# RWKV-6 attention followed by a leaky-ReLU MLP: a written-out order of all steps in place of a list scheduler

## The chip, the cores and the metric

The kernel runs on one core of a Trainium2 chip. The metric is device time in microseconds (us) from one launch to its end; lower is better. Three runs of the kernel before took 179.11, 179.33 and 179.73 us.

## What is computed

The input is a linear attention with a decaying state (4 batches, 8 heads, 768 positions, 48 channels per head), and its output, seen as 3072 tokens of 384 channels, goes through a two-layer MLP with a leaky ReLU between:

```python
for t in range(S):
    cur = np.einsum('bhd,bhe->bhde', u[None] * kt, vt)
    y[:, :, t] = np.einsum('bhd,bhde->bhe', rt, state + cur)
    state = wt[:, :, :, None] * state + np.einsum('bhd,bhe->bhde', kt, vt)
...
h = x @ w_in                      # (3072, 384) @ (384, 2048)
g = np.maximum(0.01 * h, h)
return (g @ w_out).astype(np.float32)   # (3072, 2048) @ (2048, 384)
```

## The kernel before, in words

**Tiling.** The positions are cut into chunks of 128 (24 in all, 6 for each batch). The first two chunks of batches 0 and 1 are done as two "pairs" (`pair`, chunks 0 and 1, then 2 and 3): a pair loads w, k, r and v of 256 positions with one DMA each (384 KB). All later chunks are "singles" (`single`), with four loads of 192 KB. A chunk takes the logarithm of its decays (ACT), sums them along the positions with a triangular matmul (PE), takes exponentials (ACT), scales r and k (DVE), transposes them, either on PE with a copy back or by a DMA transpose (`RK_DMA`), multiplies them (the "scores"), masks the scores (DVE, `m`), and multiplies them with v (PE, "intra"). v is cast on POOL (`vb`); POOL also makes the bonus term of u (`ru`, then `vs`). For a pair the bonus is added on PE (L808, `add_vs`). The result `y` is transposed into `xT`, the MLP's input.

**The MLP.** Chunks are joined in blocks (`blocks`, of one or two chunks). A block has "up" steps (L1157, `up`: six matmuls of 256 columns or twelve of 128, into one PSUM bank, then the leaky ReLU into `g` on ACT, L1183) and "down" steps (L1196, four matmuls of 384 columns each, four steps a chunk). The last three blocks use a seven-product scheme for their down part (`seven`, L1098). The weights arrive as float32 and are cast to bf16 by POOL, ACT or DVE (L478): `w_in` as parts in0 to in3 (384 KB each), in4 and in6 (768 KB each, two casts each), `w_out` as out0, out2, out4 and out6 (768 KB each, two casts each).

**The order of the work.** Every piece above is a "step": a closure with the engines it may run on and their planned durations, the steps it depends on, and the buffers it takes and reads. There are 1092 of them, numbered as they are made. `Plan.order` is a list scheduler: it walks through planned time, and whenever an engine is free it gives it the ready step of the lowest rank whose buffers can be had. The ranks are a base value plus an entry of `RANK`, a table of 1090 numbers; `FORCE` fixes the engine of some steps. A step's planned end is prolonged by `SLACK` (0.2 us) for most steps of the attention. The steps are then issued in the order of the plan; on the chip, each engine works through its own steps strictly in that order and waits for the others by semaphores. SyncE (SP) issues all large DMAs, in its own order too. In the first 24 us of planned time, gaps of PE are filled with matmuls on a tile of zeros (L1240).

**Buffers.** One buffer `xT` holds the transposed activations of all 24 chunks. Loads and weights go through ten `in` buffers, `g` has three, and the transposed r and k of a pair (`rkT2`) have two of their own. PSUM has eight banks (`ps`).

```python
xT = pool.tile([128, KT, NCH * L], BF16, name="xT")
make("in", 10, [128, 1536], F32)
make("rkT2", 2, [128, 2 * NP, 256], BF16)
make("g", 3, [128, NJ, max(blocks) * L], BF16)
```

Of the kernel before, what the change touches and what calls it, by code (L numbers as in the profile page):

```python
# [23 lines left out]
class Plan:  # L24


    ENGINES = ("PE", "DVE", "ACT", "POOL", "SP")
# [4 lines left out]
    def __init__(self, limits, slack_from, slack, late):  # L32
        self.steps, self.limits, self.late = [], limits, late
        self.slack_from, self.slack = slack_from, slack
# [8 lines left out]
    def order(self, pools):  # L43
        n = len(self.steps)
        users = [[] for _ in range(n)]
        left = [len(s[3]) for s in self.steps]
        for i, s in enumerate(self.steps):
            for j in s[3]:
                users[j].append(i)
        bufs = {}  # L50
        for i, s in enumerate(self.steps):
            for b in (*s[4], *s[5]):
                bufs[id(b)] = b
        remain = {k: len(b.users) for k, b in bufs.items()}
        free_tiles = {p: [(0.0, k) for k in range(len(t))] for p, t in pools.items()}
        in_use = {}
        ready_at = [0.0] * n
        self.start, self.done, self.eng = [None] * n, [0.0] * n, [None] * n
        free = dict(self.BEGIN)
        ready = {e: [] for e in self.ENGINES}  # L60
        events = []
        dma_free, flying = 0.0, []

        def offer(i, t):
            for e in self.steps[i][0]:
                heapq.heappush(events, (t, 0, e, i))

        for i in range(n):
            if not left[i]:
                offer(i, 0.0)  # L70
        for e in self.ENGINES:
            heapq.heappush(events, (free[e], 1, e, -1))
        count, out = 0, []
        while events:
            now, kind, e, i = heapq.heappop(events)
            same = {e}
            if kind == 0 and self.start[i] is None:
                heapq.heappush(ready[e], (self.steps[i][2], i))
            elif kind == 2:
                in_use[i] -= 1  # L80
            while events and events[0][0] <= now + 1e-9:
                _, kind, e, i = heapq.heappop(events)
                same.add(e)
                if kind == 0 and self.start[i] is None:
                    heapq.heappush(ready[e], (self.steps[i][2], i))
                elif kind == 2:
                    in_use[i] -= 1
            for e in self.ENGINES:
                if (e not in same and "*" not in same) or free[e] > now + 1e-9:
                    continue  # L90
                held, chosen = [], None
                while ready[e]:
                    pri, i = heapq.heappop(ready[e])
                    if self.start[i] is not None:
                        continue
                    want, ok = {}, True
                    for b in self.steps[i][5]:
                        if b.t is None:
                            want[b.pool] = want.get(b.pool, 0) + 1
                            if in_use.get(b.kind, 0) >= self.limits.get(b.kind, 99):  # L100
                                ok = False
                    for p, k in want.items():
                        if sum(f <= now + 1e-9 for f, _ in free_tiles[p]) < k:
                            ok = False
                    if ok:
                        chosen = i
                        break
                    held.append((pri, i))
                for h in held:
                    heapq.heappush(ready[e], h)  # L110
                if chosen is None:
                    continue
                i = chosen
                engs, fn, pri, deps, reads, takes, wire = self.steps[i]
                for b in takes:
                    if b.t is None:
                        slots = free_tiles[b.pool]
                        s = min(slots)
                        slots.remove(s)
                        b.slot = s[1]  # L120
                        b.t = pools[b.pool][s[1]]
                        in_use[b.kind] = in_use.get(b.kind, 0) + 1
                d = engs[e]
                self.start[i], self.eng[i] = now, e
                out.append(i)
                count += 1
                free[e] = now + d - (self.OVER[e] if d > 0.3 else 0.0)
                if wire is None:
                    self.done[i] = now + d + self.SEEN[e]
                    if self.slack_from <= pri < 1000:  # L130
                        self.done[i] += self.slack
                else:
                    wire, size, lat, lead = wire
                    while flying and sum(x for _, x in flying) + size > 150:
                        free[e] = max(free[e], flying.pop(0)[0])
                    dma_free = max(dma_free, free[e] + lead) + wire
                    flying.append((dma_free, size))
                    self.done[i] = dma_free + lat + (self.late if now > 20 else 0.0)
                heapq.heappush(events, (free[e], 1, e, -1))
                for j in users[i]:  # L140
                    left[j] -= 1
                    ready_at[j] = max(ready_at[j], self.done[i])
                    if not left[j]:
                        offer(j, ready_at[j])
                for b in {id(b): b for b in (*reads, *takes)}.values():
                    b.free_at = max(b.free_at, self.done[i])
                    remain[id(b)] -= sum(u == i for u in b.users)
                    if remain[id(b)] == 0:
                        free_tiles[b.pool].append((b.free_at, b.slot))
                        heapq.heappush(events, (b.free_at, 2, "*", b.kind))  # L150
        if count != n:
            raise RuntimeError(("stuck", count, n, [(self.steps[i][0], self.steps[i][2]) for i in range(n) if self.start[i] is None][:20]))
        return out
# [9 lines left out]
RANK = {0: -309.63, 1: -310.62, 2: -303.35, 3: -175.12, 4: -176.12, 5: -3.85, 6: -313.07, 7: -303.34, 8:  # L163
# [148 lines left out]
def kernel(  # L312
# [27 lines left out]
    MERGED = {6, 10, 12, 14, 16, 18, 20}  # L340
    LEAD = 4
    AHEAD = 4
    SLACK_FROM = 50
    SLACK = 0.2
    LATE = 0.0
    WARM_UNTIL = 24.0
# [61 lines left out]
    with tc.manual_schedule():  # L408
# [817 lines left out]
        for i, e in FORCE.items():  # L1226
            plan.steps[i][0] = {e: plan.steps[i][0][e]}
# [47 lines left out]
```

## Time and profile before

| | |
|---|---|
| three runs | 179.11, 179.33, 179.73 us (median 179.33) |
| profiled execution, first to last instruction (span) | 177.7 us; the median run is 1.6 us above it |
| busy share of the span | PE 96%, PE weight loads 75%, DVE 75%, ACT 65%, POOL 59% |
| chain that ended last | PE 74%, DMA 8%, SP's queue 5%, ACT 4%, DVE 3% |
| read from HBM, written to it | 25.17 MB, 4.72 MB |

PE is TensorE, ACT ScalarE, DVE VectorE, POOL GpSimd. PE's weight loads overlap its matmuls. A matmul's record is longer than the time until the next one starts, since matmuls are pipelined, so a busy share near 100% says that PE was never empty, not that it could do no more; the pace is read from the chain, where each piece ends with the start of the next.

### The profile page before, as it was taken

To read this page: it belongs to the slowest core of one execution; us is meant where nothing else is said; L and a number is where in the kernel's file an instruction comes from. 1 tells how busy PE (TensorE), PEld (TensorE's weight loads), DVE (VectorE), ACT (ScalarE), POOL (GpSimd) and SP (SyncE) were. 2 spreads that over 40 slices of the span, in tenths; PEclk is the share of its full clock that TensorE was granted. 3 is DMA by queue.
4 is the path that set the end of the run, shared out by engine and by line. 5 is a ranking of instruction groups with operands and counts; after the bars stand their busy time and mean duration, and the time that the engine had idled before them with its cause. 6 is when DMAs were issued, how large, how long until landed. Compare 5 with 4: busy or idle time off the path is not lost.

```text
span 177.7 us, 5379 instructions
## 1 busy us (share of the span) xinstructions
PE 170.7 (96%) x2106; PEld 133.9 (75%) x2110; DVE 133.9 (75%) x268; ACT 115.6 (65%) x258; POOL 105.3 (59%) x139
## 2 busy tenths in 40 slices
PE   7899899999999999999999999999999999999993
PEld 2456678766879767797788776788777798899992
DVE  7599744568987949979968888699779688776463
ACT  5679877764856687487497891288873677662820
POOL 5998554255897749993905994659884099100000
PEclk9999999999999999999999999999999999999999
DMA  5999999999999999997999999997999996613004
GB/s 142 262 283 341 338 377 325 234 197 168 193 146 210 171 189 191 194 227 171 221 185 209 197 147 222 205 177 155 191 208 148 241 207 160 159 24 111 4 22 157
DMA packets 115884, 34.24 MB, mean 193 GB/s; under 512 B 108305, under 2 KB 115090, under 8 KB 115858
## 3 DMA queue, kind: packets, MB, share of 16 engines
q1 hardware_dynamic: 115856, 33.89, 94.3%
q8 instruction: 16, 0.26, 0.7%
q14 instruction: 10, 0.08, 0.2%
q10 hardware_dynamic: 2, 0.00, 0.0%
HBM read 25.17 MB, written 4.72 MB: 168 GB/s over the span
## 4 chain that ended last, share of the span: by engine, by line
PE 74%; DMA 8%; SPq 5%; ACT 4%; DVE 3%; issue 3%; POOL 1%; DVEq 0%; ACTq 0%; POOLq 0%
PE ps L1168 29%; PE ps L1198 23%; PE ps L1098 8%; DMA in<-in_moe_w_in_dram 5%; SPq L630 4%; DMA in<-in_w_dram 3%; PE ps L1002 3%; PE ps L973 2%; ACT g L1183 2%; PE ps L861 2%; PE ps L556 2%; PE ps L968 2%; PE ps L942 1%; PE ps L604 1%; DVE in L1048 1%
## 5 line engine op out<-in xcount | busy, mean ns | idle before, releaser
L1168 PE MATMUL ps<-xT,w_in_b 128*128 128x256 bf16 (+1 forms) x720 | 73.3, 251 | 0.1
L1183 ACT ACTIVATE g<-ps 128x512 bf16<-128x512 f32 x96 | 55.9, 594 | 22.4 <-PE ps L1168 19.5
L1168 PEld LDWEIGHTS <-w_in_b 128*128 128x128 bf16 x720 | 57.6, 98 | 8.4 <-issue 0.3
L1198 PE MATMUL ps<-w_out_b,g 128*128 128x384 bf16 x288 | 56.5, 326 | 0.0
L1198 PEld LDWEIGHTS <-g 128*128 128x128 bf16 x288 | 25.1, 97 | 12.0
L545 DVE TENSOR_TENSOR rk<-in,ps 128x384 bf16<-128x384 f32 x48 | 25.3, 550 | 8.0 <-ACT ps L887 3.0
L575 POOL TENSOR_TENSOR ru<-in,ub 128x384 f32<-128x384 f32 x24 | 25.4, 1061 | 6.2 <-DMA in<-in_k_dram 6.1
L932 DVE TENSOR_TENSOR m<-ps,maskb 128x512 bf16<-128x512 f32 x40 | 25.3, 682 | 4.2 <-PE ps L1002 3.3
L595 POOL CAST vb<-in 128x384 bf16<-128x384 f32 x24 | 13.2, 553 | 22.3 <-DMA in<-in_v_dram 19.1
L579 POOL TENSOR_TENSOR ru<-ru,in 128x384 f32<-128x384 f32 x24 | 24.4, 1028 | 2.9 <-DMA in<-in_r_dram 2.4
L587 POOL TENSOR_TENSOR vs<-in,dg 128x384 f32<-128x384 f32 x20 | 17.0, 852 | 3.5 <-DVE dg L583 2.9
L919 POOL TENSOR_TENSOR sb<-s,a 128x384 bf16<-128x384 f32 x18 | 14.9, 830 | 3.3 <-ACT a L882 3.3
L873 DVE TENSOR_TENSOR ci<-ps,lw 128x384 f32<-128x384 f32 x20 | 11.1, 553 | 4.5 <-PE ps L861 1.8
L618 DVE TENSOR_TENSOR y<-ps,vs 128x384 bf16<-128x384 f32 x20 | 10.9, 553 | 4.5 <-PE ps L973 4.5
L583 DVE TENSOR_REDUCE dg<-ru 128x8 f32<-128x384 f32 x24 | 13.1, 544 | 0.7 <-POOL ru L579 0.6
L882 ACT ACTIVATE a<-ps 64x4 f32<-64x4 f32 x36 | 6.1, 168 | 11.6 <-DVE ci L873 8.9
L855 ACT ACTIVATE lw<-in 128x384 bf16<-128x384 f32 x20 | 10.1, 520 | 3.8 <-DMA in<-in_w_dram 3.6
L891 ACT ACTIVATE ps<-ci 128x384 f32<-128x384 f32 x20 | 9.7, 485 | 1.8 <-DVE ci L873 1.8
L887 ACT ACTIVATE ps<-ps 128x384 f32<-128x384 f32 x20 | 9.3, 467 | 0.5 <-DVE ci L873 0.3
L1240 PE MATMUL ps<-zeros 128*128 128x128 bf16 (+1 forms) x31 | 7.6, 351 | 1.6 <-DVE zeros L409 1.3
L556 PE MATMUL ps<-ident,rk 128*128 128x128 bf16 x88 | 8.4, 220 | 0.5 <-DVE rk L545 0.4
L1098 PEld LDWEIGHTS <-g 128*128 128x128 bf16 x96 | 8.1, 98 | 0.2
(105 smaller groups left out, 222.5 us busy)
## 6 DMA issues: line engine op xcount, KB each, us to landing
out_dram<-o SPq DMA_DIRECT2D x23, 192.0 KB, 2.7
in<-in_w_dram SPq DMA_DIRECT2D x20, 192.0 KB, 4.6
in<-in_v_dram SPq DMA_DIRECT2D x20, 192.0 KB, 4.9
in<-in_r_dram SPq DMA_DIRECT2D x20, 192.0 KB, 4.4
in<-in_k_dram SPq DMA_DIRECT2D x20, 192.0 KB, 4.6
in<-in_moe_w_out_dram SPq DMA_DIRECT2D x4, 768.0 KB, 8.7
in<-in_moe_w_in_dram SPq DMA_DIRECT2D x4, 384.0 KB, 7.8
in<-in_moe_w_in_dram SPq DMA_DIRECT2D x2, 768.0 KB, 8.5
```

Source lines behind the costliest of these rows:

```text
L545: (nc.gpsimd if e == "POOL" else nc.vector).tensor_tensor(out=o, in0=x, in1=i, op=ALU.mult)
L575: lambda e: nc.gpsimd.tensor_tensor(out=ru.t[:], in0=kv(), in1=ubv, op=ALU.mult),
L579: lambda e: nc.gpsimd.tensor_tensor(out=ru.t[:], in0=ru.t[:], in1=rv(), op=ALU.mult),
L583: lambda e: nc.vector.tensor_reduce(out=dg.t[:], in_=ru.t[:], axis=AX.X, op=ALU.add),
L587: lambda e: nc.gpsimd.tensor_tensor(out=vs.t[:], in0=vv(), in1=dg.t[:].unsqueeze(2).to_broadcast([128, H, D]), op=ALU.mult),
L595: {"POOL": 0.56}, lambda e: nc.gpsimd.tensor_copy(out=vb.t[:], in_=vv()),
L919: lambda e: nc.gpsimd.tensor_tensor(out=sb.t[:].rearrange("p g a d -> p (g a) d"), in0=s_in.t[:].rearrange("p g a d -> p (g a) d"), in1=a_ ...
L932: lambda e, par=par: nc.vector.tensor_tensor(out=m.t[:, par, :, :], in0=sc[par].t[:].rearrange("p (g t) -> p g t", g=NP), in1=maskb[:].uns ...
L1098: nc.tensor.matmul(o(), lhsT=x()[:, i, :], rhs=y()[:, i, :], start=fresh, stop=(stop and i == ii[-1]), skip_group_check=True)
L1168: nc.tensor.matmul(hp.t[:, a * N : (a + 1) * N], lhsT=w_in_b[:, t, (j + a) * 128 : (j + a + 1) * 128], rhs=xT[:, t, c0 : c0 + N], start=(a ...
L1183: lambda e, hp=hp, g=g, j=j, J=J, N=N: nc.scalar.activation(out=g.t[:, j : j + J, 0:N], in_=hp.t[:, 0 : J * N].rearrange("p (a n) -> p a n ...
L1198: nc.tensor.matmul(op.t[:, 0:DM], lhsT=g.t[:, j, off : off + 128], rhs=w_out_b[:, j, :], start=(j == 0), stop=(j == NJ - 1))
```

## The change

The list scheduler goes. `RANK` and `SLACK` are removed; a list `ORDER` names all 1092 steps in the order in which they are issued, and `FORCE` (64 entries before, 93 after) their engines where there is a choice. `Plan.order` only walks through `ORDER`, keeps the planned times (which decide which of several free buffers a step gets, and how many matmuls on zeros fill PE's early gaps), and hands the list back. Some planned durations are altered, which alters nothing on the chip by itself.

`xT` becomes six buffers of one block each, taken by the step that writes a block's first chunk and free again after the block's last up step. `rkT2` has no buffers of its own and uses `g`'s, of which there are four. `in` has eleven buffers.

```diff
-    def __init__(self, limits, slack_from, slack, late):
+    def __init__(self, limits):
...
+        for i in ORDER:
+            engs, fn, deps, reads, takes, wire = self.steps[i][0], *self.steps[i][1:2], *self.steps[i][3:]
+            if left[i]:
+                raise RuntimeError(("before its inputs", i))
+            e = FORCE.get(i) or next(iter(engs))
+            now = max(at[e], ready[i])
+            for b in takes:
+                if b.t is None:
+                    slot = min(free[b.pool])
...
+                    now, b.slot, b.t = max(now, slot[0]), slot[1], pools[b.pool][slot[1]]
...
-RANK = {0: -309.63, 1: -310.62, 2: -303.35, 3: -175.12, 4: -176.12, 5: -3.85, 6: -313.07, 7: -303.34, 8:
...
+ORDER = [0, 1, 4, 2, 3, 1090, 5, 6, 7, 11, 14, 20, 12, 18, 19, 13, 21, 15, 16, 17, 8, 25, 22, 36, 40, 26, 27,
...
-    xT = pool.tile([128, KT, NCH * L], BF16, name="xT")
-    make("in", 10, [128, 1536], F32)
+    make("in", 11, [128, 1536], F32)
-    make("rkT2", 2, [128, 2 * NP, 256], BF16)
-    make("g", 3, [128, NJ, max(blocks) * L], BF16)
+    make("g", 4, [128, NJ, max(blocks) * L], BF16)
+    make("xT", 6, [128, KT, max(blocks) * L], BF16)
...
+        for nb, size in enumerate(blocks):
+            xb = Buf("xT")
+            for off in range(size):
+                place[len(place)] = (xb, off * L)
...
-            return step({"ACT": 0.48, "DVE": 0.36}, xcopy, P0 + 1, deps=[s_yt], reads=[yp])
+            return step({"ACT": 0.48, "DVE": 0.36}, xcopy, P0 + 1, deps=[s_yt], reads=[yp], takes=[place[n][0]])
...
-            rkT = Buf("rkT2")
+            rkT = Buf("g", "rkT2")
...
-                                rhs=xT[:, t, c0 : c0 + N], start=(a == 0 and t == 0),
+                                rhs=xb.t[:, t, 0:N], start=(a == 0 and t == 0),
```

What this makes of the first part of each engine's queue, in short names: w0 to v0 are the loads of the first pair, w2 to v2 those of the second, w4 and so on those of single chunks; in0 to out6 are loads of weights on SP and their casts elsewhere (in4b is the second cast of in4); "b1 j8" is the up step of block 1 that begins with the 128 columns numbered 8; "down q0" is the first quarter of a chunk's down part.

| queue | before | after |
|---|---|---|
| SP, from the start | w0 k0 r0 v0 w2 in0 k2 r2 in4 in2 v2 in1 in3 out0 in6 out2 w4 out4 out6 v4 r4 k4 w5 | w0 k0 r0 w2 v0 k2 r2 in0 in4 v2 in1 in2 in3 in6 out0 w4 out2 out4 out6 k4 r4 w5 k5 v4 |
| POOL, from `vs` of the first pair | vs vs, in0, ru ru ruk ruk of the second pair, in4, vb2 vb2 vs2 vs2, in3, out0, in6, out2, out4 | vs vs, ru ru ruk ruk, in0, vb2 vb2 vs2 vs2, in1, in2, in6, out0b, out2b, out4 |
| ACT, from the second pair's exponentials | copies and casts of rkT, y and xT; in4b, g, in2, g g, in1, g, y y, g g | y y, two rkT, xT xT, in4, in4b, g g g, state, y, in3, g, in6b, g g g, out0, ln of chunk 4 |
| DVE, from the second pair's masks | four masks, dg, sb, state, xT, out0b, in6b, out2b, ci4, out4b, out6b | four masks, sb, y, xT xT, ci4, out2, out4b, out6b |
| PE, from b0 j0 | j0, j10, j8, pp2, j4, intra2, add2, bonus2, inter2, j2, yT, j6, yT, b1 j8 ... | j0, j8, pp2, j10, intra2, add2, bonus2, inter2, j2, yT, j4, yT, b1 j8 ... |

The first 61 entries of PE's queue are the same steps in both, in another order; the 61st is the same step in both, the last quarter of chunk 1's down part. Across the whole kernel DVE gets nine steps fewer and ACT nine more; PE, POOL and SP keep the number of theirs.

More of the change, by code (lines that the diff above doesn't have):

```diff
@@ L43, in order @@
     def order(self, pools):
-        n = len(self.steps)
-        users = [[] for _ in range(n)]
         left = [len(s[3]) for s in self.steps]
+        users = [[] for _ in self.steps]
         for i, s in enumerate(self.steps):
@@ L49, in order @@
                 users[j].append(i)
-        bufs = {}
-        for i, s in enumerate(self.steps):
+        remain, free = {}, {p: [(0.0, k) for k in range(len(t))] for p, t in pools.items()}
+        for s in self.steps:
             for b in (*s[4], *s[5]):
[L53 to L150, printed above, removed]
@@ L151, in order @@
-        if count != n:
-            raise RuntimeError(("stuck", count, n, [(self.steps[i][0], self.steps[i][2]) for i in range(n) if self.start[i] is None][:20]))
-        return out
+                remain[id(b)] = len(b.users)
+        n = len(self.steps)
+        self.start, self.done, self.eng, ready = [None] * n, [0.0] * n, [None] * n, [0.0] * n
+        at, in_use, wire_free, flying = dict(self.BEGIN), {}, 0.0, []
+        for i in ORDER:
[7 more added lines that the diff above has]
+                    slot = min(free[b.pool])
+                    free[b.pool].remove(slot)
+                    in_use[b.kind] = in_use.get(b.kind, 0) + 1
+                    if in_use[b.kind] > self.limits.get(b.kind, 99):
+                        raise RuntimeError(("too many", b.kind, i))
+                    now, b.slot, b.t = max(now, slot[0]), slot[1], pools[b.pool][slot[1]]
+            self.start[i], self.eng[i] = now, e
+            at[e] = now + engs[e] - (self.OVER[e] if engs[e] > 0.3 else 0.0)
+            if wire is None:
+                self.done[i] = now + engs[e] + self.SEEN[e]
+            else:
+                time, size, lat, lead = wire
+                while flying and sum(x for _, x in flying) + size > 150:
+                    at[e] = max(at[e], flying.pop(0)[0])
+                wire_free = max(wire_free, at[e] + lead) + time
+                flying.append((wire_free, size))
+                self.done[i] = wire_free + lat
+            for b in {id(b): b for b in (*reads, *takes)}.values():
+                b.free_at = max(b.free_at, self.done[i])
+                remain[id(b)] -= sum(u == i for u in b.users)
+                if not remain[id(b)]:
+                    free[b.pool].append((b.free_at, b.slot))
+                    in_use[b.kind] -= 1
+            for j in users[i]:
+                left[j] -= 1
+                ready[j] = max(ready[j], self.done[i])
@@ L156 @@
+        if len(set(ORDER)) != n or len(ORDER) != n:
+            raise RuntimeError(("order", n, len(ORDER)))
+        return ORDER
 LOAD = (1.1, 64, 1.4, 0.2)
@@ L493, in weight_steps, with columns @@
                 (win_s if which == 0 else wout_s).append(step(
-                    {"DVE": 1.0 if which == 0 else 0.66, "ACT": 0.83, "POOL": 1.0}, cast, pri + 1, deps=[ld], reads=[st]))
+                    {"DVE": 1.3 if which == 0 else 0.6, "ACT": 0.83, "POOL": 0.86 if which == 0 else 0.96}, cast, pri + 1, deps=[ld], reads=[st]))
         xt_steps, lns, firsts, rows = {}, {}, {}, {}
+        place = {}
+        for nb, size in enumerate(blocks):
+            xb = Buf("xT")
+            for off in range(size):
+                place[len(place)] = (xb, off * L)
+        def columns(n):
+            xb, off = place[n]
+            return lambda: xb.t[:, :, off : off + L]
         prev = [None] * B
@@ L1049, in mix @@
                 last = done[x] = step(
-                    {"DVE": 1.2}, sub, MIX_RANK, deps=[*wout_s, last], reads=t[: x // 2 + 1], takes=[t[x // 2]])
+                    {"DVE": 1.43}, sub, MIX_RANK, deps=[*wout_s, last], reads=t[: x // 2 + 1], takes=[t[x // 2]])
             mixed.extend([part, t, done])
@@ L1157 @@
             N = size * L
-            c0 = chs[0] * L
+            xb = place[chs[0]][0]
             g = Buf("g")
```

56 lines of the change are left out of this document (24 added, 32 removed), and 188 rows, old and new, of tables (ORDER, RANK).

## The prediction

> **What bounds the kernel now.** I read the page first, then the busy time by stretch, then the chain of waits for PE's pace, then the timeline of each engine where PE has holes.
>
> ```profile
> span 177.7 us, 5379 instructions
> PE 170.7 (96%) x2106; PEld 133.9 (75%) x2110; DVE 133.9 (75%) x268; ACT 115.6 (65%) x258; POOL 105.3 (59%) x139
> 0.00:24.00 24.00, 20.49 (x298) 12.67 (x302) 18.53 (x48) 17.22 (x34) 19.29 (x37) 1.00 1.06 281
> 24.00:36.00 12.00, 12.00 (x154) 10.31 (x153) 5.42 (x9) 9.57 (x18) 4.20 (x5) 1.00 1.06 298
> 36.00:150.00 114.00, 113.50 (x1373) 87.91 (x1371) 93.29 (x175) 76.44 (x183) 80.15 (x96) 1.00 1.08 189
> 150.00:174.80 24.80, 24.72 (x290) 22.96 (x287) 16.38 (x39) 12.39 (x25) 1.67 (x2) 1.00 0.29 81
> L1240 PE MATMUL ps<-zeros 128*128 128x128 bf16 (+1 forms) x31 | 7.6, 351 | 1.6 <-DVE zeros L409 1.3
> 174.76 0.36 DVE L1119 TENSOR_TENSOR o<-ps,o 128x192 f32<-128x192 f32 x1 [0.30 <-PE ps L1098]
> ```
>
> The four lines from 0.00 on are stretches of the span: length, then busy us of PE, PE's weight loads, DVE, ACT and POOL, the granted clock, the DMA engines' share, GB/s. PE is the bound: from 24.0 to 174.8 us it is idle for 12.00 - 12.00 + 114.00 - 113.50 + 24.80 - 24.72 = 0.58 us. The granted clock is 1.00 throughout. Only the first 24 us have room: 24.00 - 20.49 = 3.5 us idle and 7.6 us of matmuls on zeros. After the last add (last line) only a store is left, and the change keeps both.
>
> A busy record is longer than the time a matmul holds PE, so I looked for small holes by pace:
>
> ```profile
> 26.05 1.34 PE ps L1168 x24
> 27.39 0.65 PE ps L1198 x4
> 77.03 1.31 PE ps L1168 x12
> 65.22 0.82 PE L1198 MATMUL ps<-w_out_b,g 128*128 128x384 bf16 x4
> 66.35 0.33 PE L942 MATMUL ps<-vb,rk 128*128 128x96 bf16 x4 [0.31 <-ACT g L1183]
> 126.69 1.46 PE L1198 MATMUL ps<-w_out_b,g 128*128 128x384 bf16 x8
> 127.78 0.93 ACT L855 ACTIVATE lw<-in 128x384 bf16<-128x384 f32 x2
> 128.35 0.32 PE L861 MATMUL ps<-lw,trev 128*128 128x384 bf16 x1 [0.19 <-ACT lw L855]
> ```
>
> The first three are pieces of the chain: 24 up matmuls of 128 columns in 1.34 us (56 ns each), 4 down ones in 0.65 (162 ns), 12 of 256 columns in 1.31 (109 ns). At that pace the four at 65.22 end at 65.87, and the next starts at 66.35: 0.48 us lost, behind a leaky ReLU that held the PSUM bank. The eight at 126.69 end at 127.99, the next starts at 128.35: 0.36 lost to a logarithm. These 0.84 us are the largest holes of the steady part.
>
> The number and size of the real matmuls do not change. So the change can gain at most part of the first 24 us and these small holes, and can lose by new ones.
>
> **The start, step by step.** PE's hole of the start lies ahead of the second pair's state sums (L727, "pp2"):
>
> ```profile
> 18.20 0.81 PE L1168 MATMUL ps<-xT,w_in_b 128*128 128x256 bf16 x6
> 19.06 1.47 PE L1168 MATMUL ps<-xT,w_in_b 128*128 128x256 bf16 x12
> 21.69 0.47 PE L727 MATMUL ps<-vb,rk 64*128 64x96 bf16 x14 [0.23 <-POOL vb L595]
> 22.09 0.83 PE L1168 MATMUL ps<-xT,w_in_b 128*128 128x256 bf16 x6
> 24.24 0.82 PE L1168 MATMUL ps<-xT,w_in_b 128*128 128x256 bf16 x6
> 10.09 0.96 POOL L595 CAST vb<-in 128x384 bf16<-128x384 f32 x2
> 15.25 1.98 POOL L579 TENSOR_TENSOR ru<-ru,in 128x384 f32<-128x384 f32 x2
> 20.68 0.96 POOL L595 CAST vb<-in 128x384 bf16<-128x384 f32 x2 [1.80 <-DMA in<-in_v_dram]
> 21.60 1.61 POOL L587 TENSOR_TENSOR y<-in,dg 128x384 bf16<-128x384 f32 x2
> 23.16 0.82 POOL L488 CAST w_in_b<-in 128x768 bf16<-128x768 f32 x1
> 10.55 0.84 ACT L644 ACTIVATE lw<-in 128x768 bf16<-128x768 f32 x1 [0.17 <-DMA in<-in_w_dram]
> 21.76 0.83 ACT L492 CAST w_in_b<-in 128x768 bf16<-128x768 f32 x1 [0.41 <-DMA in<-in_moe_w_in_dram]
> 17.97 2.47 DVE L780 TENSOR_TENSOR m<-ps,mask 128x512 bf16<-128x512 f32 x4
> ```
>
> The two up steps at 19.06 were over by 20.53, and pp2's bulk began at 21.69: a hole of 1.16 us, in part under matmuls on zeros. POOL stood idle 1.80 us for v2, which landed at 20.68. In1 was next in SP's queue and landed at 21.76, so 384 KB of weights cost the queue 1.08 us. After the change in2 no longer goes ahead of v2, and what else goes ahead is the same: v2 lands at 20.68 - 1.08 = 19.60. POOL has no other work in between (in4's cast has gone to ACT). Its casts of v2 end at 19.60 + 0.96 = 20.56, and pp2, which began 0.05 us after that cast's end, begins at 20.61.
>
> From 21.69 to 24.24 PE did pp2, one up step, intra, add, bonus, inter, in 2.55 us. After the change the same six kinds stand there, so the next up step (j2) can begin at 20.61 + 2.55 = 23.16. Its weights are cast by POOL behind v's two products: 20.61 - 0.05 - 0.04 + 1.56 = 22.08 (0.05 and 0.04 lead back to the start of the products, as 21.69 to 21.60; 1.56 is from 21.60 to 23.16), + 0.82 = 22.90, in time. That is 1.08 us earlier than 24.24, but one up step (12 in 1.31, so 0.66) has moved from ahead of pp2 to behind it. **Net gain 1.08 - 0.66 = 0.42 us.**
>
> What is delayed, and its cover: w2 has gone ahead of v0. w2 landed at about 10.5 (the logarithm waited for it), so v0 now lands about then, and POOL's cast at 10.09 slips by 0.4 us, with all that POOL does behind it: the products that ended at 17.23 end at 17.6, in0's cast (0.82) at 18.45, and the first up step begins near 18.5 in place of 18.20. Two up steps of 0.66 from there end by 20.0, ahead of pp2's 20.61: the cover is 0.6 us, and whatever goes over it comes off the gain one for one. The four masks end at 20.44 before; with one more copy (0.42) and 0.4 us of slip they end by 21.3, needed at 20.61 + 0.40 + 0.66 = 21.67. If ACT is late, with the copies of y and xT moved to it from DVE, the same 0.6 us cover it. So the start gives between -0.3 (both slips beyond the cover) and +1.0 (no hole left: 0.42 and the 0.6 of cover); I take 0.4, nearest to the row with the wait of 1.80. The matmuls on zeros are placed anew by the plan; one that stands where PE is not idle costs at most its mean of 0.35.
>
> **From there to 37 us** the weights' arrival could take the gain back:
>
> ```profile
> 37.27 0.39 PE L556 MATMUL ps<-ident,rk 128*128 128x128 bf16 x4
> 25.00 0.83 POOL L488 CAST w_out_b<-in 128x768 bf16<-128x768 f32 x1 [1.02 <-DMA in<-in_moe_w_out_dram]
> 27.02 0.83 POOL L488 CAST w_in_b<-in 128x768 bf16<-128x768 f32 x1 [1.20 <-DMA in<-in_moe_w_in_dram]
> 29.22 0.56 DVE L490 CAST w_out_b<-in 128x768 bf16<-128x768 f32 x1 [0.83 <-DMA in<-in_moe_w_out_dram]
> 32.21 0.83 POOL L488 CAST w_out_b<-in 128x768 bf16<-128x768 f32 x1 [1.75 <-DMA in<-in_moe_w_out_dram]
> 30.11 0.52 ACT L855 ACTIVATE lw<-in 128x384 bf16<-128x384 f32 x1
> 34.47 0.56 DVE L490 CAST w_out_b<-in 128x768 bf16<-128x768 f32 x1 [1.02 <-DMA in<-in_moe_w_out_dram]
> ```
>
> Behind the first row, the start of the 62nd PE step, these are the landings of out0, in6, out2, out4 and out6, and ACT's first use of w4, which came next after out2. After the change in6 and out0 swap places (24.95 and 27.0), w4 goes ahead of out2 (which then lands by 30.1), the last two stay. The first 61 entries of PE's queue are the same steps in both kernels, and the 61st ended at 37.27 before, so at 36.85 now. Counted back from there at 0.65 a step, the first step that needs out2 begins at 36.85 - 5 x 0.65 = 33.6, out4 at 34.9, out6 at 36.2. Each lies later than landing plus cast (30.9, 33.0, 35.3). The tightest has 0.9 us, less if ACT takes three activations ahead of its cast. The gain holds to 37 us, and a start gain of over 1.3 us would be cut here.
>
> **The steady part.** From 37 us on, only new or vanished holes count. The 0.84 us of the two holes are of one old order; the new one meets the same two kinds of wait at other places. Bounds: all 0.84 gone, or 1.0 us of new ones (twice the 0.48). DVE gives nine steps to ACT, at 93.29 of 114 us against 76.44, and `g`'s fourth buffer frees block starts, so I take 0.5 gained. The buffers of `xT`: a block's buffer is next taken six blocks later, when its up steps are long done, so this wait costs nothing; its cover is five blocks of PE work of 2.6 us and more each, and without it the copy would wait at most for one block's up steps, 2.6 to 5.2 us. The eleventh `in` buffer adds at most one load in flight, while DMA runs at a share of 1.08. The scores, masks and stores are the same in number: nothing.
>
> **Sum.** 0.4 + 0.5 = 0.9 us off this execution's span, 177.7 to 176.8. The median run lies 179.33 - 177.7 = 1.6 us above that span and I keep it: 178.4 us. What a measurement of this kernel can tell from no change is about 0.3%, 0.54 us.
>
> **Rivals.**
>
> (a) More is gained: no hole is left at the start (1.0) and both steady holes go (0.84): 179.33 - 1.84 = 177.5. For it: DVE, the engine with the least idle time beside PE, loses steps. Against: the first up step still waits for in0 and the copies.
>
> (b) Nothing to measure: the start's 0.4 goes into slips, the steady holes only change places. 179.1, with 0.4 on either side. For it: PE's 0.58 us idle in 151.
>
> (c) Slower. The plan's allowance of 0.2 us is gone, and the order is fixed ahead for loads whose landing varies:
>
> ```profile
> in<-in_w_dram SPq DMA_DIRECT2D x20, 192.0 KB, 4.6
> 55.41 6.14 DMA in<-in_w_dram
> ```
>
> The median load of w lands 4.6 us after its issue, the one in the chain took 6.14. If PE's queue reaches a chunk's sum when its load is late by that 1.54 us, PE stops, since its queue goes on in order, as it did for 0.36 us at 128. One full hit with the start's gain kept: 179.33 - 0.4 + 1.5 = 180.4. It decides from 0.95 us of new waits in all. For it: DMA at 1.08. Against: the waits of ACT for w are few and short, and PE's queue holds MLP steps in between.
>
> (d) A cast at the head of ACT's queue. ACT waited 0.41 us at 21.76 for a weight with activations behind it. The new order puts in6's second cast ahead of three activations; if in6 lands at 27.02 as before and not at 24.95, these wait 2.07 us, and PE stops when all eight PSUM banks wait for ACT. Between 0 and 2.07 us; half of it gives 179.33 - 0.4 + 1.0 = 179.9.
> The Trainium skill (TensorE: Matmul & The Clock Gate, section "Architectural detail: the array is 16× 32×32, not 1× 128×128") has ACT and DVE as strict FIFOs, and TensorE alone able to pull weight loads forward; by that rule the moved casts can only harm whatever stands behind them. The row at 21.76 agrees: the wait was ACT's own.
>
> **Chances.** My forecast (177.9 to 178.7) 0.45, (a) 0.12, (b) 0.18, (c) 0.18, (d) 0.07. Faster by over 0.3%: 0.45 + 0.12 = 0.57. Within 0.3%: 0.18. Slower: 0.25. The range reaches from just below (a) to just above (c): 177.2 to 180.5; what falls outside is a sum of several hits, or more than every hole known.
>
> **What would show it.** Right: POOL's wait for v2 ends near 19.6 and pp2 starts near 20.6; the 61st PE step ends near 36.9; PE idle after 24 us is at most 0.6 us. Wrong: v2 lands at 20 or later; the first up step starts after 18.9; a PE wait of over 0.5 us on ACT's logarithm or on a leaky ReLU between 37 and 150 us; or PE's last matmul, before at 174.7, later than 174.2.

## The result: 184.53 us, slower by 3%

The changed kernel takes 184.53 us (median of 4 runs, 184.45 to 185.87), the kernel before 179.53 in the same series (179.11 to 180.42): a ratio of 1.0302, with a 95% interval of 1.0254 to 1.0349. The prediction said 178.4, at most 180.5. The profiled execution took 184.62 us, its span 182.9. Runs with a granted clock of 0.985 to 0.991 (one of these four, three of six in e1 and in e3 below) took about 1.5 us longer than those at 0.998 or more, where the changed kernel lies at 184.45 to 184.62 us, e1 at 182.84 to 183.15 and e3 at 184.18 to 184.35.

The page after, then busy time by stretch (length, then PE, weight loads, DVE, ACT, POOL, clock, DMA, GB/s), then single rows of the timelines, as far as they answer to those of before:

```profile
span 182.9 us, 5361 instructions
PE 171.4 (94%) x2105; PEld 134.1 (73%) x2108; DVE 128.9 (70%) x259; ACT 118.1 (65%) x267; POOL 103.8 (57%) x139
0.00:24.00 24.00, 19.26 (x291) 11.88 (x294) 17.82 (x46) 15.85 (x34) 19.30 (x37) 1.00 1.06 282
24.00:36.00 12.00, 12.00 (x157) 10.47 (x154) 4.54 (x9) 11.32 (x22) 4.20 (x5) 1.00 1.04 294
36.00:150.00 114.00, 112.57 (x1349) 86.61 (x1348) 84.57 (x158) 77.25 (x184) 73.00 (x90) 1.00 1.06 177
150.00:178.90 28.90, 27.55 (x314) 25.13 (x313) 21.64 (x48) 13.68 (x30) 7.36 (x8) 1.00 0.44 113
...
8.16 1.95 DVE L404 TENSOR_TENSOR rk<-in,ps 128x384 bf16<-128x384 f32 x4 [2.22 <-ACT a L538]
13.89 0.34 PE L529 MATMUL ps<-ones,lw 64*128 64x1 bf16 x8 [0.95 <-ACT ps L548]
19.55 0.96 POOL L454 CAST vb<-in 128x384 bf16<-128x384 f32 x2 [1.50 <-DMA in<-in_v_dram]
20.29 1.48 PE L1027 MATMUL ps<-xT,w_in_b 128*128 128x256 bf16 x12
21.71 0.52 PE L588 MATMUL ps<-vb,rk 64*128 64x96 bf16 x16
24.34 0.82 PE L1027 MATMUL ps<-xT,w_in_b 128*128 128x256 bf16 x6
38.02 0.61 PE L415 MATMUL ps<-ident,rk 128*128 128x128 bf16 x8
176.84 2.35 DVE L978 TENSOR_TENSOR o<-ps,o 128x192 f32<-128x192 f32 x7
```

The real matmuls are the same, so the 5.2 us between the spans can be located. The 62nd PE step starts at 38.02, before at 37.27: the start lost 0.75 us. From 36 us to the last matmul PE is idle for 1.43 + 1.35 = 2.8 us, before for 0.58. The last add ends at 179.19, before at 175.12, so 4.1 us are gone by then, 3.3 of them after the start; from there to the end of the span 3.7 us pass, before 2.6. The loads are not late: POOL's wait for v2 ends at 19.55, as forecast.

Some of what the engines wait for has grown. These are rows of the waits (total us, times, longest), of the kernel before and then of the changed one. `ci` (DVE, L873 before, now L733) adds the logarithms to a chunk's cumulative sums, `a` (ACT, L882, now L742) takes the exponential of its column sums; L747 is the exponential `er`, which does need `ci`:

```profile
ACT a L882 <- DVE ci L873: 8.9, 14, 2.1
DVE ci L873 <- ACT a L882: 1.0, 1, 1.0
ACT a L677 <- DVE rk L545: 0.7, 1, 0.7
```

```profile
ACT ps L747 <- DVE ci L733: 10.8, 14, 2.4
DVE ci L733 <- ACT a L742: 7.4, 12, 1.3
DVE rk L404 <- ACT a L538: 2.2, 1, 2.2
PE ps L1027 <- ACT a L742: 0.8, 1, 0.8
```

`ci` and `a` have no step of each other among their inputs: each depends on the chunk's cumulative sums alone. Both read one PSUM bank, `ci` its first 384 columns and `a` four columns behind them. In both kernels the one that stands later in the list waits for the other, and the list decides who. Before, both `a` stood behind `ci` in 14 of 18 chunks; in the new list at least one `a` stands ahead in all 18. The same holds for `a2` and `rk2` of a pair (third row of each fence).

How such a wait reaches PE, in the timeline at 153 us:

```profile
151.49 0.56 DVE L733 TENSOR_TENSOR ci<-ps,lw 128x384 f32<-128x384 f32 x1 [1.28 <-ACT a L742]
152.08 0.48 ACT L747 ACTIVATE ps<-ps 128x384 f32<-128x384 f32 x1 [0.62 <-DVE ci L733]
152.59 1.02 DVE L404 TENSOR_TENSOR rk<-in,ps 128x384 bf16<-128x384 f32 x2 [0.54 <-ACT ps L747]
153.18 0.17 ACT L742 ACTIVATE a<-ps 64x4 f32<-64x4 f32 x1 [0.22 <-DVE rk L404]
153.40 0.82 PE L1027 MATMUL ps<-xT,w_in_b 128*128 128x256 bf16 x6 [0.79 <-ACT a L742]
```

`ci` waits for the first `a`, the exponential and `rk` for `ci`, the second `a`, which the list puts behind, for `rk`, and PE for the bank.

I took this as theory S: users of one PSUM bank on different engines wait for each other in the order of the list, readers too, and the plan behind the list knows no such wait. Rival O: the list is simply too tight for loads and engines that come late (the prediction's rival (c)). Rival D: ACT's longer queue.

### The profile page after: what moved, and what is told of

Same layout as the page of the kernel before. It is cut to its first block, busy times and chain, and to the rows that moved or that the text cites. A ratio compares the mean times of both kernels' runs of the same rounds, so it can differ in the third digit from the quotient of the medians.

```text
span 182.9 us, 5361 instructions
## 1 busy us (share of the span) xinstructions
PE 171.4 (94%) x2105; PEld 134.1 (73%) x2108; DVE 128.9 (70%) x259; ACT 118.1 (65%) x267; POOL 103.8 (57%) x139
## 4 chain that ended last, share of the span: by engine, by line
PE 63%; DVE 10%; ACT 9%; POOL 5%; issue 4%; DMA 4%; SPq 1%; DVEq 0%; POOLq 0%
PE ps L1027 24%; PE ps L1057 18%; PE ps L957 6%; DMA in<-in_v_dram 4%; ACT g L1042 3%; PE ps L861 2%; PE ps L415 2%; DVE ci L733 2%; PE ps L833 2%; DVE rk L404 2%; POOL ru L434 2%; ACT ps L548 1%; DVE o L978 1%; POOL sb L779 1%; PE ps L828 1%
## 5 line engine op out<-in xcount | busy, mean ns | idle before, releaser
L1027 PE MATMUL ps<-xT,w_in_b 128*128 128x256 bf16 (+1 forms) x720 | 72.1, 251 | 0.8 <-ACT a L742 0.8
L1042 ACT ACTIVATE g<-ps 128x512 bf16<-128x512 f32 x96 | 54.6, 605 | 20.5 <-PE ps L1027 18.8
L1057 PE MATMUL ps<-w_out_b,g 128*128 128x384 bf16 x288 | 55.3, 326 | 0.0
L1057 PEld LDWEIGHTS <-g 128*128 128x128 bf16 x288 | 25.9, 97 | 12.9
L434 POOL TENSOR_TENSOR ru<-in,ub 128x384 f32<-128x384 f32 x24 | 23.9, 998 | 15.7 <-DMA in<-in_k_dram 15.3
L404 DVE TENSOR_TENSOR rk<-in,ps 128x384 bf16<-128x384 f32 x48 | 24.7, 550 | 10.9 <-ACT ps L747 5.0
L733 DVE TENSOR_TENSOR ci<-ps,lw 128x384 f32<-128x384 f32 x20 | 11.1, 557 | 13.0 <-ACT a L742 7.4
L454 POOL CAST vb<-in 128x384 bf16<-128x384 f32 x24 | 12.4, 523 | 9.6 <-DMA in<-in_v_dram 7.2
L747 ACT ACTIVATE ps<-ps 128x384 f32<-128x384 f32 x20 | 9.4, 471 | 10.9 <-DVE ci L733 10.8
L472 ACT COPY xT<-ps 128x384 bf16<-128x384 bf16 x12 | 5.7, 490 | 5.9 <-PE ps L465 5.9
L415 PE MATMUL ps<-ident,rk 128*128 128x128 bf16 x88 | 7.7, 220 | 1.8 <-DVE rk L404 1.8
L817 DVE TENSOR_TENSOR s<-ps,sb 128x384 f32<-128x384 f32 x14 | 7.7, 550 | 1.3 <-PE ps L802 1.3
```

The lines of the kernel that those rows point to most:

```text
L404: (nc.gpsimd if e == "POOL" else nc.vector).tensor_tensor(out=o, in0=x, in1=i, op=ALU.mult)
L434: lambda e: nc.gpsimd.tensor_tensor(out=ru.t[:], in0=kv(), in1=ubv, op=ALU.mult),
L454: {"POOL": 0.56}, lambda e: nc.gpsimd.tensor_copy(out=vb.t[:], in_=vv()),
L733: lambda e: nc.vector.tensor_tensor(out=ci.t[:], in0=heads(cp.t), in1=lw.t[:, :, 0:D], op=ALU.add),
L1027: nc.tensor.matmul(hp.t[:, a * N : (a + 1) * N], lhsT=w_in_b[:, t, (j + a) * 128 : (j + a + 1) * 128], rhs=xb.t[:, t, 0:N], start=(a == 0 ...
L1042: lambda e, hp=hp, g=g, j=j, J=J, N=N: nc.scalar.activation(out=g.t[:, j : j + J, 0:N], in_=hp.t[:, 0 : J * N].rearrange("p (a n) -> p a n ...
```

## The experiments

Each is given with its ratio to the kernel before, measured in the same series (1.0302 is the changed kernel's).

**e1: `ci` ahead of `a` in all 18 chunks.** Only the list between engines changes:

```diff
-229, 232, 231, 230, 233
+229, 230, 232, 231, 233
```

> The changed kernel; in the list of steps each of the 18 single chunks' ci (DVE, L733) is put ahead of its two a (ACT, L742), where the changed kernel has it behind the first of them. Both only read the same PSUM bank. The order within each engine's own queue, the buffers and the zeros stay as they are. Theory S (the framework makes the reader that stands later in the list wait for the other one, though both only read): ci no longer waits for a, and with that the waits behind it shrink, at 48.3 (0.60), 52.4 (0.39), 105 to 109 (0.65), 149.8 (0.33) and 153.4 (0.79): 181.4 to 182.8 us from 184.5; the start and the end stay as they are. Rival O (the fixed order meets loads or engines late, whatever the list says between engines): 184.2 to 184.8, the same holes in PE behind other releasers. Rival D (copies moved from DVE to ACT lengthen ACT's queue): 184 to 184.8, with ACT still named at the holes.

183.78 us, ratio 1.0247 (1.0206 to 1.0287): faster than the changed kernel, but short of what S expected (181.4 to 182.8). The wait has changed sides:

```profile
ACT a L794 <- DVE ci L785: 13.0, 15, 2.2
POOL sb L831 <- ACT a L794: 10.2, 4, 4.7
```

Now `a` waits for `ci`, and `er` stands behind the two `a` in ACT's queue, so 2 x 0.17 us pass between `ci` and `er`. A swap can only choose which of the two waits; whether the shared bank itself is what costs is for e5 to test.

**e2: the same for the first pair.**

```diff
-15, 16, 17, 8, 25, 22
+15, 8, 25, 16, 17, 22
```

> The changed kernel; in the list of steps the first pair's first rk product (step 25, DVE) is put ahead of the two a2 exponentials (steps 16 and 17, ACT) that read the same PSUM bank; nothing else, and no engine's own queue. Theory S: the first rk begins at about 7.0 us instead of 8.16, and PE's lag behind the kernel before at 24 us falls from 0.77 to 0.3 or less: 183.5 to 184.1 us. Rival O: rk is released by something else at about 8.1, 184.4 to 184.8 us. A case between: rk begins early, but the masks and the first up steps (20.3 us) wait for tot2 (0.95 us, behind an exponential on ACT) all the same, and the time stays at 184.3 or more.

183.54 us, ratio 1.0240 (1.0213 to 1.0268).

```profile
7.40 1.95 DVE L456 TENSOR_TENSOR rk<-in,ps 128x384 bf16<-128x384 f32 x4 [1.47 <-PE ps L581]
```

`rk` starts at 7.40 in place of 8.16, the 62nd PE step at 37.26, as early as in the kernel before (37.27), and the last matmul ends 0.6 us earlier (178.18 after 178.80). So the start's loss was this one swap, as S says, although the wait of 0.95 us for the pair's sums (PE L581) behind an exponential is still there. That `rk` doesn't reach 7.0 is the sums' own write into the same bank: PE does it at 6.96, in the kernel before at 6.57.

**e3: seven `o` buffers.**

```diff
-    make("o", 5, [128, DM], F32)
+    make("o", 7, [128, DM], F32)
```

> The changed kernel with seven o buffers instead of five. Theory T (at the end the copies of the second projection's results wait for an o buffer that a store still holds: 4.14 us idle ahead of the copy at 176.29, and PE waits 0.35 for it at 176.66): 183.5 to 184.2 us from 184.5, the last matmul at 178.2 or earlier. Rival: the end is set by the order of the adds on DVE and of the products on PE, and the last matmul is as late: 184.4 to 184.8.

184.91 us, ratio 1.0323 (1.0281 to 1.0365), and the last matmuls start at 177.94, in the changed kernel at 177.97: theory T falls. The copy that PE waits for starts at the same time (176.25 after 176.29), and its row now names what it waited for:

```profile
176.25 0.32 ACT L973 COPY o<-ps 128x192 f32<-128x192 f32 x1 [4.09 <-DVE o L978]
```

An add on DVE that reads the other half of the same bank: theory S again, at a place where I had looked for a store.

**e4: the converse in the kernel before.** `a` ahead of `ci` in all chunks:

```diff
-210, 211, 212
+211, 212, 210
```

> The kernel before; in its list of steps each single chunk's two a (ACT, L882) are put ahead of its ci (DVE, L873), as the changed kernel has them; 14 of the 18 chunks stand the other way in the kernel before. Engines' own queues, buffers and zeros are unchanged. Theory S: ci waits for a as in the changed kernel, and the time rises by 1 to 3 us, to 180.5 to 182.5. Rivals O and D: no change, 179.2 to 179.9.

179.36 us, ratio 1.0003 (0.9987 to 1.0019), though the waits are there:

```profile
DVE ci L925 <- ACT a L934: 9.7, 15, 1.5
```

A miss for S as I had put it: 9.7 us of this wait cost the old list nothing. So the direction alone costs nothing; my guess was that it depends on the room that the list leaves behind the wait.

To see whether that can carry the whole loss I worked both lists out once more on paper: each engine takes its steps in order, with the plan's own durations, once without and once with the rule that users of one bank on different engines wait for each other in the list's order. PE then ends at 173.5 and 173.7 for the old list, at 173.0 and 179.1 for the new one (measured: 174.7 and 178.8), and the new holes lie at 48.4, 109.4, 150.8, 154.1 and 177.1 us. That is a calculation and no measurement, but it says what to try: take away the sharing.

**e5: no shared bank for `ci` and `a`.** The list is the changed kernel's. The sums that `a` reads go into the bank of the exponential `ek`, which is taken earlier for it, so that two such banks may be held at once.

```diff
-                        cp.t[:, DM + p : DM + p + 1],
+                        ek.t[:, DM + p : DM + p + 1],
-                        ... in_=cp.t[q0 : q0 + 64, DM : DM + NP], func=AF.Exp),
+                        ... in_=ek.t[q0 : q0 + 64, DM : DM + NP], func=AF.Exp),
```

> The changed kernel, its list of steps untouched; the column sums that a reads are written into the chunk's ek bank (taken at the cumulative sums instead of at the ek exponential, with room for two ek banks), so that a (ACT, L742) and ci (DVE, L733) no longer share a PSUM bank and neither order between them makes one wait. Theory S, widened (the first experiments showed that a behind ci costs nearly as much as ci behind a, because er follows both): the holes in PE at 48.3, 52.4, 105 to 109, 149.8 and 153.4 go, 181.3 to 182.3 us from 184.5. Rival O (the list is late for other reasons): 183.3 or more, like the swap of the two alone (183.8).

182.07 us, ratio 1.0193 (1.0155 to 1.0231), in the band of S (181.3 to 182.3). The row of `ci` waiting for `a` is gone, and PE's idle time from 36 to 150 us falls from 1.43 to 0.54 us:

```profile
36.00:150.00 114.00, 113.46 (x1367) 87.94 (x1365) 83.93 (x160) 79.24 (x189) 74.68 (x93) 1.00 1.07 179
```

**e6: the pairs too.**

```diff
-                            cg.t[:, DM + g : DM + g + 1],
+                            tt.t[:, DM + g : DM + g + 1],
```

> As the run before, and in the two pairs the sums that a2 reads get a PSUM bank of their own, so that tot2 no longer waits for the exponential over its bank and rk2 no longer for a2. Theory S: also the start's 1.2 us of late rk and the 0.95 us of tot2 go, PE's lag at 24 us is below 0.1: 179.6 to 180.8 us. Rival O: 182.5 or more.

181.49 us, ratio 1.0134 (1.0106 to 1.0162): in the direction of S, 0.7 us above its band (179.6 to 180.8).

```profile
20.61 0.51 PE L589 MATMUL ps<-vb,rk 64*128 64x96 bf16 x16
36.92 0.61 PE L415 MATMUL ps<-ident,rk 128*128 128x128 bf16 x8
36.00:150.00 114.00, 112.72 (x1360) 87.33 (x1359) 84.78 (x160) 79.48 (x188) 74.86 (x93) 1.00 1.05 178
```

The start did what S says and more: pp2 starts at 20.61 and the 62nd PE step at 36.92, in e5 at 37.82. But PE's idle time from 36 to 150 us grows from 0.54 to 1.28 us: much of what the start gains is lost again behind it. What was left is in e7 to e14.

**e7: two adds at the end ahead of the products that write their bank.**

```diff
-1035, 1036, 1073, 1072, 1040, 1043, 1068, 1074, 1069, 1075, 1077, 1037, 1076, 1088
+1035, 1036, 1037, 1073, 1072, 1040, 1043, 1068, 1074, 1069, 1075, 1076, 1088, 1077
```

> As the run before, and at the end of the list two adds on DVE (1037 and 1076) move ahead of the PE products (1043 and 1077) that write other columns of the bank they read. Theory S: the wait of the copy 1078 for 1076 goes, and PE's 0.35 us ahead of product 1082 with it: 0.2 to 0.4 us below the run before, 179.3 to 180.6 us. Rival: the end is set by stores and their landing, no difference to the run before.

180.73 us, ratio 1.0093 (1.0066 to 1.0119). That is 0.76 us below e6, more than the 0.2 to 0.4 expected, and 0.13 above the band, which started from a lower e6. The copy starts with the product's end, PE's hole of 0.35 us is gone, and the last store leaves earlier after the last add.

**e8: the old list in the new buffers.**

```diff
-ORDER = [0, 1, 4, 2, 3, 1090, ...
+ORDER = (the 1092 steps as the kernel before issues them; FORCE: its engines)
```

> The changed kernel's code and buffers (eleven in buffers, six xT, four g) with the list of steps and the engines that the kernel before comes to. Theory S: the buffers cost nothing and the loss lies in the order alone, 179.0 to 180.2 us; the end after the last matmul (2.95 us in the kernel before, 4.1 in the changed one) goes with the order, 3.0. Rival B (the buffers' new places or the longer program cost time): above 180.6 us, or an end of 4.1 us with the old order too.

178.99 us, ratio 1.0012 (0.9987 to 1.0038). The buffers cost nothing; all of the loss is in the order and the choice of engines, the end after the last add included. That end, in rows of e8, e7 and e9 (span, and last add):

```profile
span 177.9 us, 5385 instructions
174.96 0.36 DVE L972 TENSOR_TENSOR o<-ps,o 128x192 f32<-128x192 f32 x1 [0.30 <-PE ps L951]
```

```profile
span 179.2 us, 5374 instructions
175.42 0.36 DVE L979 TENSOR_TENSOR o<-ps,o 128x192 f32<-128x192 f32 x1 [0.30 <-PE ps L958]
```

```profile
span 178.4 us, 5387 instructions
175.34 0.36 DVE L981 TENSOR_TENSOR o<-ps,o 128x192 f32<-128x192 f32 x1 [0.30 <-PE ps L960]
```

From the end of the last add to that of the span: 2.6 us with the old list, 3.4 in e7, 2.7 in e9.

**e9: e7 with longer streams on POOL and SP.**

```diff
+            if i == PADS:
+                for x in range(9):
+                    nc.gpsimd.memset(ones_f[0:1, x : x + 1], 1.0)
+                for x in range(6):
+                    nc.sync.dma_start(out=pad[0:1, 16 * x : 16 * x + 16], in_=w[0, 0, x : x + 1, 0:16])
```

> The kernel of e7 with nine tiny memsets on POOL and six loads of 64 bytes on SP added in mid run, into places that nothing reads afterwards. In all runs with the changed kernel's list the stretch from the last store's landing to the end of the span took 1.80 us, in all with the old list 0.91 to 0.94; two closing instructions, one on SP and one on POOL, take longer there. Theory K (which instruction of SP's and POOL's streams falls on a place that has to be fetched; the old list has 3 to 6 more on SP and 9 more on POOL): with the streams longer by as many, the stretch is 0.9 to 1.1 us and the time 179.6 to 180.2 from 180.73. Rival W (something still open at the end, a transfer or a semaphore that the new list leaves late): 1.8 us as before, 180.5 to 181.1.

180.03 us, ratio 1.0047 (1.0027 to 1.0067): 15 instructions that do nothing make the kernel shorter by 0.7 us, the amount by which the closing fell (3.4 to 2.7). Theory K's forecast came true. That fetching is the mechanism is not shown by it, only that these additions to the two streams decide; the last section has what the traces add.

**e13: the last shared banks.** In e9 three chunks still have one:

```profile
46.05 0.55 DVE L406 TENSOR_TENSOR rk<-in,ps 128x384 bf16<-128x384 f32 x1 [1.66 <-ACT a L745]
147.21 0.17 ACT L745 ACTIVATE a<-ps 64x4 f32<-64x4 f32 x1 [0.68 <-DVE rk L406]
```

```diff
+            ts = Buf("ps", "ts") if n in (6, 22, 23) else ek
-                        ek.t[:, DM + p : DM + p + 1],
+                        ts.t[:, DM + p : DM + p + 1],
```

> The kernel of e9; in three chunks (6, 22 and 23), whose second a stands in the list behind the product that reads their ek bank, the sums get a bank of their own. What is left of shared banks in e9 shows as rk waiting 1.66 us for a at 46.05 and a waiting 0.68 for rk at 147.2. Theory S: those two waits and the holes of 0.42 and 0.31 us in PE behind them go, 179.2 to 179.8 us from 180.03. Rival O (late loads and bare lack of slack set what is left): 179.9 or more.

179.59 us, ratio 1.0024 (1.0012 to 1.0036); both rows are gone. The interval still touches e9's, so the size is less sure than the disappearance.

**e14: one sum on DVE behind the chain of the next chunk.** The cause, in e9:

```profile
70.96 1.00 POOL L440 TENSOR_TENSOR ru<-ru,in 128x384 f32<-128x384 f32 x1 [1.20 <-DMA in<-in_r_dram]
71.99 0.55 DVE L444 TENSOR_REDUCE dg<-ru 128x8 f32<-128x384 f32 x1 [0.58 <-POOL ru L440]
73.04 0.47 ACT L750 ACTIVATE ps<-ps 128x384 f32<-128x384 f32 x1 [0.98 <-DVE ci L736]
74.62 0.40 PE L417 MATMUL ps<-ident,rk 128*128 128x128 bf16 x4 [0.37 <-DVE rk L406]
```

```diff
-346, 347, 825, 333, 335, 336, 334, 337, 338, 339, 340, 349
+346, 825, 333, 335, 336, 334, 337, 338, 339, 340, 347, 349
```

> As the run before, and on DVE the sum over one chunk's ru (step 347), which waits at about 72 us for a POOL product whose r load lands 1.2 us after POOL is ready, moves behind the ci and the two rk products that stand after it in DVE's queue. Rival O's share (a load that lands later than the list assumes holds DVE's queue): the hole of 0.53 us in PE at 74 goes, 0.3 to 0.6 us below the run before. If it is no load that makes that hole, no difference to the run before.

178.97 us, ratio 0.9998 (0.9987 to 1.0009). The r load is still 0.86 us late for POOL, but `ci` starts at 71.44 and no longer behind it:

```profile
70.92 1.00 POOL L440 TENSOR_TENSOR ru<-ru,in 128x384 f32<-128x384 f32 x1 [0.86 <-DMA in<-in_r_dram]
71.44 0.56 DVE L737 TENSOR_TENSOR ci<-ps,lw 128x384 f32<-128x384 f32 x1 [0.17 <-PE ps L725]
```

So rival O has its share: one late load, about 0.5 us. Rival D cannot carry the loss: e14 keeps the changed kernel's engines, the nine more steps on ACT included, and runs as fast as the kernel before.

**e10: the old list with own banks** (e8 with the sums of `a` and of `a2` each in a bank of their own).

```diff
-            cp = Buf("ps", "cp")
+            cp, ts = Buf("ps", "cp"), Buf("ps", "ts")
-                        cp.t[:, DM + p : DM + p + 1],
+                        ts.t[:, DM + p : DM + p + 1],
```

> The old list and engines in the changed kernel's buffers (as e8), with banks of their own for the sums that a and a2 read. Theory S: the old list, in which 14 of 18 chunks have ci first and PE is nearly always covered, pays little for the shared banks: 0.2 to 0.8 us below e8, 178.2 to 178.8. Rival: the shared banks cost the old list nothing, 178.8 to 179.3.

178.24 us, ratio 0.9946 (0.9930 to 0.9962): faster than both kernels. PE has no idle time left after 24 us:

```profile
36.00:150.00 114.00, 114.00 (x1385) 89.09 (x1383) 94.23 (x177) 78.25 (x184) 80.97 (x97) 1.00 1.11 190
150.00:173.70 23.70, 23.70 (x278) 21.97 (x275) 15.09 (x35) 11.86 (x24) 0.00 (x0) 1.00 0.28 78
```

**e11 and e15: lists searched anew** with the bank rule in the model, own banks in both; e11 from e7's list, e15 from e10's.

```diff
-ORDER = (the list of e7; of e10)
+ORDER = (the same steps, found by moving single steps while the worked-out end falls)
```

> The kernel of e7 (own banks) with the list of steps searched anew from e7's, by a replay in which users of one PSUM bank on different engines wait for each other in the order of the list, and loads may land 0.7 us late. Theory S: without waits that its model doesn't know, the list keeps its promise; the replay ends 1.1 us before e7's and 0.7 before the kernel before's: 177.8 to 179.6 us (the upper part if the closing takes 1.8 us). Rival O (any list searched so tightly is late on the chip): above 180.

> The kernel of e10 (old engines, own banks) with its list searched a little further by the same replay, steps that share a buffer kept in their order: the replay ends 0.35 us before e10's. Theory S: 177.7 to 178.4 us. Rival O: above e10's 178.24 by more than 0.3.

e11: 179.07 us, ratio 1.0000 (0.9985 to 1.0015). e15: 178.55, ratio 0.9957 (0.9942 to 0.9972). e11 is within its band, e15 0.15 us above it, and neither beats e10: the 0.35 us that the calculation promised e15 did not arrive. With own banks and the bank rule in the model, a searched list no longer loses 5 us, but the model isn't exact to 0.3 us either. A third list, searched from the old one (e12), makes the kernel compute something else, so its 179.01 us is no evidence.

## Why the prediction was wrong, step by step

The steps that held: v2's landing (19.60 forecast, 19.55 measured), the swap of in6 and out0 and the other weight landings up to 37 us, and the buffers at no cost (e8). Rival (d) did not occur: in6 landed early, as the main line had it.

**The start failed at "the first up step begins near 18.5".** It began at 20.29, so the cover of 0.6 us was exceeded by 1.2, pp2 began at 21.71 and not 20.61, and the 0.42 gained became 0.75 lost. The weights were not the reason: in0's cast ended at 18.05, ahead of the forecast 18.45. I followed the loads and POOL's queue and took ACT, DVE and PE's order among themselves as neutral. Two waits were new: `rk` for `a2` (2.22 us, start 8.16 in place of 7.00) and the pair's column sums (tot2) for an exponential over their bank (0.95). e2 took away the first alone and gave back all of the 0.75 us at the 62nd PE step. With both gone (e6) pp2 began at 20.61 and that step at 36.92, close to the forecast's 20.61 and 36.85, although the first up step began at 19.19: so the rest of this part's sum held, and the bank waits were what it lacked. The third waits row of before, `a2` waiting 0.7 us for `rk`, was this very wait from its other side.

**The steady part failed at "only new or vanished holes count" with its bounds of -1.0 to +0.84.** From the 62nd PE step to the last add 3.3 us were lost. I bounded new holes by twice the largest old one, as if their number were drawn by chance. They had one cause, present in each of 18 chunks, and it stood in the waits of before: `a` 8.9 us behind a `ci` that it doesn't need. I didn't ask why a step waits for one that is not among its inputs, and didn't look which of the two the new list puts first. With the sharing gone (e5, e6, e13) the ratio falls from 1.0302 to 1.0193, 1.0134 and, e7 and e9 in between, from 1.0047 to 1.0024: about 2 + 1 + 0.4 us.

The Trainium skill (PSUM — Partial Sum Buffer, section "PSUM bank collisions raise a hardware error ⚠️") says why the wait is there: ACT and DVE on the same bank and partitions collide even if both only read, at whatever columns, so software has to keep them apart. The waits rows agree that they are kept apart here; no run lets them meet.

**The end failed at "only a store is left, and the change keeps both".** The last add came 4.1 us late, but 1.1 us more were lost behind it, about 0.2 by the last store's place in SP's queue and the rest in the closing (e7, e9).

**Rival (c)** had a true mechanism and the wrong weight: one late load that DVE's queue passes on, worth about 0.5 us (e14), where I gave it 1.5 and had it, beside the cast of (d), as the only way to be slower. The condition "from 0.95 us of new waits" was met by another wait.

**The forecast's size.** With the bank waits, the closing and the late load taken out (e14), the new list runs at 178.97 us, ratio 0.9998. So even then the 0.9 us of gain weren't there. The start's part was: PE's 62nd step begins at 36.72, 0.55 us ahead of before. The steady part's 0.5 was not: PE is idle for 0.65 us from 36 to 150 us, before for 0.50, and 0.5 of it is one wait for a transposing DMA.

That the old list loses only 0.7% to the same sharing (1.0012 in e8, 0.9946 in e10) and the new one nearly 2% is shown; why is not. That its planner's allowance of 0.2 us made the room is my reading; no run changed the allowance alone.

## What to carry to other kernels

When a row shows a step waiting for one that is not among its inputs, find the resource that they share, before any reordering; a planner that doesn't know that wait can promise time that doesn't exist, as it did here. If the share is a few columns in a PSUM bank, give them a bank of their own: it was worth 0.7% in the old list and nearly 2% in the new. An order fixed ahead needs a spot check of each queue for a step that waits for a load with the critical chain behind it.

## What the runs showed of the hardware

The stretch from the last store's landing to the end of the span took 1.80 us in the changed kernel and 0.92 in the kernel before. Two closing instructions make the difference: one on SP and one on POOL each start about 0.3 us later behind the one ahead of them, and take 0.12 and 0.21 us in place of 0.01 and 0.08. Nine memsets and six tiny loads in mid run, on POOL and SP, brought most of that back: the stretch is 1.06 us in e9, and neither instruction is slow there. The Trainium skill (Runtime: NRT & Kernel Launch, section "Instruction fetch mechanics") has each engine fetch its instructions in blocks of 256 and calls the crossing of a block mostly hidden; a crossing that falls into the closing, where nothing hides it, would fit. The traces record transfers of instructions: in the changed kernel two of 8 KB start 0.64 and 0.69 us after the two slow instructions do, in e7 0.65 and 0.70. In the kernel before and in e9 none starts behind the last landing, but in e8 and e10, with short stretches (0.94 and 0.93 us), one does. So that the two instructions wait for a fetch is likely and not shown.
